# Two decode layers on one core: the weights and cache in 76 loads instead of 90

## The chip, the cores and the metric

The kernel runs on one core of a Trainium2 chip. The metric is the device time of one execution in microseconds (us); before the change it is 732.17 us, the median of 3 runs (731.61 to 732.62). A matrix unit (PE, with its weight loads listed as PEld), a vector engine (DVE), a scalar engine (ACT) and the queue engine SP, which only issues loads here, each work through their own instructions in order and wait for each other on semaphores.

## What is computed

Four tokens (one for each of 4 sequences) pass an attention layer and a gated MLP, and then the same two again with the same weights and the same cache:

```
x = x + A(layernorm(x));  x = x + B(layernorm(x))      # and once more
A: q = x @ wq                      # 640 -> 32 heads of 128
   k, v = last 1024 cached rows    # 4 x 32 heads x 1024 x 128, fp32
   o = softmax(q k^T / sqrt(128)) v;   return o @ wo
B: g = x @ W_gate; g = g * (g > 0);   return (g * (x @ W_up)) @ W_down   # 640 -> 1728 -> 640
```

Everything is fp32. Each layer needs all 32 heads' keys and values (each head's 4096 columns of 128 rows of either), the projections and the MLP's 25,920 columns; only what fits on chip is kept from the first layer to the second.

## The kernel before

The host lays the data out as three arrays of 128 rows. `heads` holds, in the order of use, the query weights ("q"), keys ("k"), values ("v") and output weights ("o") of heads 0 to 26; `kept` holds those of heads 27 to 31, as 3,200 columns of "o", 3,200 of "q" (the kept W_q) and 40,960 of keys and values; `mlp` holds the MLP's weights: 1,920 columns for the last piece of gate and up weights, three blocks of 5,120 for the rest, and then the down weights. A column is 512 bytes over the 128 rows.

On chip there is one buffer `store` of 50,624 columns and a small `first_q` for the first 4,288 columns of `heads`. A list `plan` is written out by hand in `decode_kernel`: every entry says which layer it is for, from which array, which columns, and where in `store` they go. `load()` takes the next entry as soon as the kernel's text has passed the last use of the columns that it overwrites, and issues one load on SP's queue (L221). On the chip, that load waits until the last instruction that uses any of its target columns is done. So a load of two pieces in one waits for the later of their two release times, and who uses it waits until all of it has landed.

The order of the work: layer 1 goes through the common heads in groups of four (last, a group of three), and then through the kept heads (27 to 31). The kept keys and values stay in `store`, where layer 2 starts with them, so that while the first MLP and the start of layer 2 run, only a narrow part of `store` is free: 3,264 columns behind the kept ones (from `FRONT`), and three small stretches (`AHEAD`, `AWAY`, `BACK`), whose kept contents are moved aside to PSUM and small tiles for that time. The first MLP's loads go round these places, layer 2's first loads also; as layer 2 works off the kept heads, the places behind them come free, and the loads grow ("first stretch", L182 to L199). Then come loads of about 15,872 columns round `store` (`stretch`), the last heads, and the second MLP, cut in `cuts` (L204).

In an MLP (`forward`), `gate(3)` multiplies with the 1,920 columns, `gate(0)` to `gate(2)` with a block of 5,120 each, and `gated(j)` makes one block's hidden values on ACT and DVE, for which the next block's matmuls wait. `down(3)`, `down(0)`, `down(1)`, `down(2)` follow; each multiplies one hidden block with 640 columns at a time. All matmuls with loaded data are issued by `product` (L252). `normalized` makes the layer norm and the turned input xT, with a few idle matmuls (`busy`, `fill`) beside it; in the second layer's MLP, there are none after `gate(3)`.

Of the kernel before, what the change touches and what calls it, by code (L numbers as in the profile page):

```python
# [13 lines left out]
B, D, H, DH, W, F = 4, 640, 32, 128, 1024, 1728  # L14
# [12 lines left out]
KV = 4096  # L27
# [4 lines left out]
KEPT = len(HEADS[K0]) + len(HEADS[K1])  # L32
# [19 lines left out]
GU0, GU = KC * 3 * P, KC * 4 * 256  # L52
WD0 = GU0 + 3 * GU
TAIL, WD1, WD = WD0 + D, WD0 + D + 2 * QUARTER, 4 * D
MLP = WD1 + 3 * WD
# [6 lines left out]
STORE = 50624  # L62
FRONT = KEPT * 2 * (D + KV)


AHEAD = KEPT * D, KEPT * D + 768
BACK = FRONT - 2 * KV - 1728, FRONT - 2 * KV
AWAY = BACK[0] - 1280, BACK[0]
HOME = 12864
FIRST, MOST = 32640, 16320  # L70
# [7 lines left out]
def fewest(lo, end, n):  # L78

    if n == 1:  # L80
        return (0, [end]) if end - lo <= MOST else (n + len(CUTS), [])
    most = min(lo + MOST, end)
    ends = [(most, most not in CUTS)] + [(x, False) for x in CUTS if most - 512 < x < most]
    return min((fewest(hi, end, n - 1)[0] + cut, [hi, *fewest(hi, end, n - 1)[1]]) for hi, cut in ends)


def spread(parts):


    at, places, cuts = 0, {}, [0]  # L90
    for what, i in parts:
        places[what, i] = at
        size = size_of(what, i)
        step = {"q": size // KC, "k": 512, "v": 512, "o": D}[what]
        cuts += range(at + step, at + size + 1, step)
        at += size
    return places, at, cuts


ROWS = {row: spread(parts) for row, parts in PARTS.items()}  # L100

CUTS = frozenset(ROWS["heads"][2])
fewest = cache(fewest)
WHERE = {part: (row, at) for row, (places, _, _) in ROWS.items() for part, at in places.items()}

# [2 lines left out]
def decode_kernel(ctx: ExitStack, tc: tile.TileContext, x, source, sel, out):  # L108
    nc = tc.nc
# [10 lines left out]
    store = big.tile([P, STORE], F32, name="store")  # L120
# [9 lines left out]
    def put(layer, row, to, *cuts):  # L130

        for lo, hi in zip(cuts, cuts[1:]):
            assert 0 < hi - lo <= MOST and to % 64 == lo % 64 == hi % 64 == 0 and to + hi - lo <= STORE, (row, lo, hi, to)
            plan.append((layer, row, lo, hi, to))
            to += hi - lo
        return to

    def stretch(layer, lo, end, to):

        for hi in fewest(lo, end, -(-(end - lo) // MOST))[1]:  # L140
            if to + hi - lo > LAP:
                to = 0
            to = put(layer, "heads", to, lo, hi)
            lo = hi
        return to

    def at_part(what, i):
        return WHERE[what, i][1]

    def near(c, row="heads"):  # L150

        return max(x for x in ROWS[row][2] if x <= c)

    heads_end = ROWS["heads"][1]
    k0, v0 = at_part("k", HEADS[K0][0]), at_part("v", HEADS[K0][0])
    k1, v1 = at_part("k", HEADS[K1][0]), at_part("v", HEADS[K1][0])


    q_end = 2 * KEPT * D
    turn = min(c for c in ROWS["heads"][2] if c >= heads_end - (STORE - q_end))  # L160
    mid = [near(turn + (heads_end - turn) * i // 3) for i in (1, 2)]
    to = stretch(0, HELD, turn, FIRST)
    assert to <= KEPT * D or to > 2 * MOST, to
    put(0, "kept", KEPT * D, KEPT * D, q_end)
    put(0, "heads", q_end, turn, *mid, heads_end)
    put(0, "kept", k0, k0, k1, v0, v0 + 6656, v1, v1 + KV, v1 + 7168, FRONT)
    put(0, "kept", 0, 0, len(HEADS[K0]) * D, KEPT * D)


    f, z, a, q, k = FRONT, STORE - D, AHEAD[0], AWAY[0], BACK[0]  # L170
    assert STORE - FRONT == 2 * 1280 + 64 + D
    gu = [(z, D), (f, 1280), (f + 1280, 1344), (a, 768), (k, 960), (k + 960, 768), (q, 1280)]
    gu_end = [(f, 1280), (f + 1280, 1280), (f + 2560, D)]
    wd = [(a, D), (k, 960), (k + 960, D), (q, 1280), *gu_end, (a, D), (k, D), (k + D, D)]
    lo = 0
    for to, n in gu + gu + gu_end + wd:
        put(0, "mlp", to, lo, lo + n)
# [2 lines left out]


    lo = HELD  # L182
    for to, n in (f, 1280), (f + 1280, 1280), (f + 2560, D + 64), (a, 768), (k, 1728):
        put(1, "heads", to, lo, lo + n)
        lo += n
    to = AHEAD[1]
    for n in 1152, 1280, 1024, 2048, 3392:
        to = put(1, "heads", to, lo, lo + n)
        lo += n
    assert to == HOME  # L190
    to = HOME + BACK[1] - BACK[0]
    for n in 4096, 6144, 9728:
        hi = near(lo + n)
        to = put(1, "heads", to, lo, hi)
        lo = hi
    hi = near(lo + 4608)
    to = put(1, "heads", to, lo, hi)
    lo, hi = hi, near(hi + STORE - to)
    put(1, "heads", to, lo, hi)  # L199
    last = near(heads_end - 25216)  # L200
    to = stretch(1, hi, last, 0)
    for lo, hi in (last, near(last + 12800)), (near(last + 12800), heads_end):
        to = put(1, "heads", to if to + hi - lo <= STORE else 0, lo, hi)
    cuts = [0, 7040, 12160, GU0 + 3 * GU, WD1 + WD, MLP - 4 * D, MLP - 2 * D, MLP - D, MLP]  # L204
    for lo, hi in zip(cuts, cuts[1:]):
        to = put(1, "mlp", to if to + hi - lo <= STORE else 0, lo, hi)

# [2 lines left out]
    live = [False] * STORE  # L210
    held = {}

    def load():

        if not held:
            nc.sync.dma_start(out=first_q, in_=source["heads"][:, :HELD])
        while plan and not any(live[plan[-1][4]:plan[-1][4] + plan[-1][3] - plan[-1][2]]):
            layer, row, lo, hi, to = plan.pop()
            live[to:to + hi - lo] = [True] * (hi - lo)
            held.setdefault((layer, row), []).append((lo, hi - lo, to))  # L220
            nc.sync.dma_start(out=store[:, to:to + hi - lo], in_=source[row][:, lo:hi])  # L221

    def free(a, b):
        live[a:b] = [False] * (b - a)
        load()
# [29 lines left out]
    def done(layer, row, lo, n):  # L255

        if row == "kept" and layer == 0:
            return
        if row == "kept":
            for p in range(lo, lo + n):  # L260
                if BACK[0] <= p < BACK[1]:
                    live[HOME + p - BACK[0]] = False
                elif not (AHEAD[0] <= p < AHEAD[1] or HOME <= p < HOME + BACK[1] - BACK[0]):
                    live[p] = False
        else:
            for first, m, p in held[key(layer, row)]:
                a, b = max(lo, first) - first, min(lo + n, first + m) - first
                if a < b:
                    live[p + a:p + b] = [False] * (b - a)
        load()  # L270
# [8 lines left out]

    probs = work.tile([P, W], F32, name="probs")  # L280
    load()
    gates = work.tile([P, 512], F32, name="gates")
    sel_sb = const.tile([P, P + 32], F32, name="sel_sb")
# [390 lines left out]
```

## Time and profile before

| | |
|---|---|
| median of 3 runs | 732.17 us (731.61 to 732.62) |
| profiled execution, first to last instruction (its span) | 729.8 us |
| bytes read | 310.57 MB |
| loads on SP's queue | 90, and one store |
| PE busy, share of the span | 60% |
| mean granted PE clock | 0.822 |

The profile gives no other time of the profiled execution than its span, 729.8 us; the median of the timed runs lies 2.3 us above it, for what the span does not hold. The tables of the profile give busy times by engine, the chain of waits that ended last, and, for chosen stretches of time, the busy time of each engine, the granted PE clock and the rate of the loads.

### The profile page before, as it was taken

The page shows a single profiled execution, that of the slowest core. Times are in us where ns is not written, and L with a number is a line of the kernel's source. Part 1 is how long each engine was busy: PE and PEld are TensorE (multiplying, and loading weights), DVE is VectorE, ACT ScalarE, POOL GpSimd, SP SyncE. Part 2 cuts the span into 40 slices and gives each one's busy share as a digit, 9 for nine tenths or more (in the row PEclk, how much of TensorE's full clock was granted, in tenths as well). Part 3 has the DMA queues.
Part 4 walks back from the last instruction along what each step waited for, and adds up shares of the span by engine and source line. Part 5 has one row for each costly group of instructions (what it writes and reads, how often), then busy time and mean ns, then how long its engine had stood idle before and what let it go on. Part 6 is the DMA issues. An engine that isn't in the chain of part 4 may idle for free.

```text
span 729.8 us, 8270 instructions
## 1 busy us (share of the span) xinstructions
PE 437.2 (60%) x3764; PEld 143.9 (20%) x3764; DVE 76.7 (11%) x277; ACT 54.2 (7%) x101; POOL 0.3 (0%) x5
## 2 busy tenths in 40 slices
PE   0745565555646664619868896365656556555575
PEld 0211111111111111103333241021111112111132
DVE  1111001010010101001111211001010010101011
ACT  0200000000000000000412210000000000000100
POOL 0000000000000000000000000000000000000000
PEclk9888888876777777759999999677777777878899
DMA  9999999999999999999999999999999999999996
GB/s 409 442 398 443 442 443 416 438 440 439 418 439 432 411 460 421 447 416 426 419 407 401 434 429 449 445 425 435 425 435 443 429 434 427 441 433 430 421 425 289
DMA packets 13290, 311.17 MB, mean 426 GB/s; under 512 B 1476, under 2 KB 1732, under 8 KB 6984
## 3 DMA queue, kind: packets, MB, share of 16 engines
q1 hardware_dynamic: 13104, 310.56, 99.0%
q8 instruction: 29, 0.48, 0.2%
q10 hardware_dynamic: 152, 0.09, 0.1%
q14 instruction: 5, 0.04, 0.0%
HBM read 310.57 MB, written 0.08 MB: 426 GB/s over the span
## 4 chain that ended last, share of the span: by engine, by line
DMA 76%; PE 21%; another core or an unknown queue 1%; DVE 1%; issue 1%; SPq 0%; ACT 0%; DVEq 0%; ACTq 0%
DMA store<-in_heads 60%; PE ps L252 9%; DMA store<-in_kept 8%; DMA store<-in_mlp 7%; PE po L252 5%; PE m L252 2%; PE y L252 1%; PE pp L252 1%; PE pp L432 1%; PE m L403 1%; PE m L472 0%; PE m L463 0%; PE m L345 0%; PE y L375 0%
## 5 line engine op out<-in xcount | busy, mean ns | idle before, releaser
L252 PE MATMUL po<-store,pT 128*16 128x512 f32 (+1 forms) x1026 | 155.3, 709 | 123.6 <-DMA store<-in_heads 118.2
L252 PE MATMUL ps<-store,qT 128*4 128x512 f32 (+4 forms) x996 | 150.4, 684 | 109.8 <-DMA store<-in_heads 89.2
L252 PEld LDWEIGHTS po<-store,pT 128*16 128x16 f32 x1026 | 34.2, 109 | 230.3 <-issue 109.2
L252 PEld LDWEIGHTS ps<-store,qT 128*4 128x4 f32 x996 | 29.9, 93 | 213.4 <-DMA store<-in_heads 100.3
L424 DVE TENSOR_REDUCE nm<-ps 128x1 f32<-128x1024 f32 x17 | 20.8, 1225 | 240.7 <-PE ps L252 240.7
L428 ACT ACTIVATE probs<-ps,nm 128x1024 f32<-128x1024 f32 x17 | 18.9, 1114 | 327.0 <-DVE nm L424 327.0
L252 PE MATMUL m<-store,xT 128*32 128x512 f32 (+4 forms) x150 | 28.4, 570 | 11.0 <-DMA store<-in_heads 11.0
L442 DVE COPY pT<-pp 128x16 f32<-128x16 f32 x128 | 17.1, 169 | 137.8 <-PE po L252 137.8
L252 PE MATMUL y<-store,oT 128*4 128x160 f32 x514 | 22.6, 307 | 9.9 <-DMA store<-in_heads 8.7
L459 ACT COPY gates<-po 128x512 f32<-128x512 f32 x16 | 9.4, 587 | 252.4 <-PE po L252 252.4
L252 PE MATMUL pp<-store,xT 128*32 128x256 f32 (+3 forms) x322 | 20.1, 350 | 8.7 <-DMA store<-in_mlp 4.3
L432 PE MATMUL pp<-sel_sb,probs 128*128 128x128 f32 x144 | 20.7, 291 | 0.0
L465 DVE RECIPROCAL r<-m 128x16 f32<-128x16 f32 x18 | 4.6, 258 | 132.9 <-PE m L463 132.9
L432 PEld LDWEIGHTS pp<-sel_sb,probs 128*128 128x128 f32 x144 | 18.3, 153 | 0.0
L252 PEld LDWEIGHTS y<-store,oT 128*4 128x4 f32 x514 | 12.7, 88 | 17.5 <-DMA store<-in_heads 9.1
L396 DVE TENSOR_SCALAR gates<-m,rstd 128x512 f32<-128x512 f32 (+2 forms) x18 | 12.4, 690 | 24.9 <-PE m L252 24.9
L252 PEld LDWEIGHTS pp<-store,xT 128*32 128x32 f32 x322 | 10.3, 109 | 17.0 <-DMA store<-in_mlp 7.7
L472 PE MATMUL m<-sel_sb,gates 128*128 128x128 f32 x72 | 11.9, 287 | 0.8 <-DVE gates L452 0.8
L403 PE MATMUL m<-sel_sb,gates 128*128 128x128 f32 x64 | 12.3, 315 | 0.0
L322 PE MATMUL y<-probs,sel_sb 4*4 4x160 f32 x8 | 0.7, 444 | 18.2 <-DMA sel_sb<-in_sel 18.2
L403 PEld LDWEIGHTS m<-sel_sb,gates 128*128 128x128 f32 x64 | 7.6, 155 | 18.3 <-issue 17.9
L252 PE MATMUL y<-store,gates 128*4 128x160 f32 x192 | 9.6, 299 | 2.5 <-DMA store<-in_mlp 2.3
(74 smaller groups left out, 126.1 us busy)
## 6 DMA issues: line engine op xcount, KB each, us to landing
store<-in_heads SPq DMA_DIRECT2D x17, 7936.0 KB, 46.1
store<-in_heads SPq DMA_DIRECT2D x2, 8160.0 KB, 44.7
store<-in_heads SPq DMA_DIRECT2D x2, 8128.0 KB, 36.1
store<-in_heads SPq DMA_DIRECT2D x2, 7968.0 KB, 36.1
store<-in_heads SPq DMA_DIRECT2D x1, 8096.0 KB, 26.4
store<-in_heads SPq DMA_DIRECT2D x1, 7424.0 KB, 44.9
store<-in_heads SPq DMA_DIRECT2D x1, 7360.0 KB, 35.8
store<-in_heads SPq DMA_DIRECT2D x1, 7168.0 KB, 34.0
```

The lines of the kernel that those rows point to most:

```text
L252: nc.tensor.matmul(out[:, a:z], by, t[rows, p:p + z - a], start=start and not a, stop=stop and z == n, **how)
L322: nc.tensor.matmul(y[32 * g:32 * g + B], ident[:B, :B], probs[:B, g * QUARTER:(g + 1) * QUARTER], start=True, stop=True, tile_position=(0, ...
L396: nc.vector.tensor_scalar(gates[:, :len(HEADS[g]) * P], qp.pop(g), rstd, SCALE, op0=ALU.mult, op1=ALU.mult)
L403: nc.tensor.transpose(qt[:, i], gates[:, i * P:(i + 1) * P], ident)
L424: nc.vector.tensor_reduce(nm[g], to.rearrange("p j n -> p (j n)"), axis=AX.X, op=ALU.max, negate=True)
L428: nc.scalar.activation(probs, sc.pop(g).rearrange("p j n -> p (j n)"), AF.Exp, bias=nm.pop(g), accum_out=sums[g])
L432: nc.tensor.transpose(pp[:, c // 4, c % 4 * P:c % 4 * P + P], probs[:, c * P:(c + 1) * P], ident)
L442: nc.vector.tensor_copy(to[:, 4 * j:4 * j + 4], pp[:, j].rearrange("p (c x) -> p c x", c=4)[:, :, i:P:32])
L459: nc.scalar.copy(gates, po)
L465: nc.vector.reciprocal(r[g], so.rearrange("p (b i) -> p i b", b=B)[:, :SIDE])
L472: nc.tensor.transpose(ot[:, 127 * b:127 * b + P], gates[:, b * P:(b + 1) * P], ident)
```

## The change

Three groups of loads are put together; no byte more or less is read, and no arithmetic changes.

1. The kept W_q (3,200 columns) were a load of their own in layer 1. Now the host also writes them into the array `heads`, in front of the load of the last common heads at `turn`, and that load brings both. The three loads there become nearly equal.
2. The first MLP is loaded in 19 pieces instead of 27 (640 + 1,280 columns become 1,920, 960 + 768 become 1,728, and so on), and layer 2's first stretch in 11 instead of 15.
3. The second MLP's first cut falls away: the 1,920 columns and the first two blocks of 5,120 come in one load of 12,160 columns, instead of 7,040 and 5,120. The last heads' loads of layer 2 are cut at other columns, four as before.

```
+QUERIES = min(c for c in CUTS if c >= ROWS["heads"][1] - (STORE - 2 * KEPT * D)), KEPT * D
...
-    put(0, "kept", KEPT * D, KEPT * D, q_end)
     put(0, "heads", q_end, turn, *mid, heads_end)
-    put(0, "kept", k0, k0, k1, v0, v0 + 6656, v1, v1 + KV, v1 + 7168, FRONT)
+    put(0, "kept", k0, k0, k1, v0, v0 + 6656, v1, v1 + 5120, v1 + 7168, FRONT)
...
-    gu = [(z, D), (f, 1280), (f + 1280, 1344), (a, 768), (k, 960), (k + 960, 768), (q, 1280)]
-    gu_end = [(f, 1280), (f + 1280, 1280), (f + 2560, D)]
-    wd = [(a, D), (k, 960), (k + 960, D), (q, 1280), *gu_end, (a, D), (k, D), (k + D, D)]
+    gu = [(f, 1920), (f + 1920, 1344), (a, 768), (k, 1728), (q, 1280)]
+    gu_end = [(f, 1920), (f + 1920, 1280)]
+    wd = [(a, D), (k, 1600), (q, 1280), *gu_end, (a, D), (k, 1280)]
...
-    for n in 1152, 1280, 1024, 2048, 3392:
+    for n in 2432, 3072, 3392:
...
-    for n in 4096, 6144, 9728:
+    for n in 4096, 8192:
...
-    hi = near(lo + 4608)
+    hi = near(lo + 12288)
...
-    last = near(heads_end - 25216)
-    to = stretch(1, hi, last, 0)
-    for lo, hi in (last, near(last + 12800)), (near(last + 12800), heads_end):
+    to = stretch(1, hi, turn, 0)
+    last, end = near(turn + MOST), near(heads_end - 12608)
+    for lo, hi in (turn, last), (last, end), (end, heads_end):
...
-    cuts = [0, 7040, 12160, GU0 + 3 * GU, WD1 + WD, MLP - 4 * D, MLP - 2 * D, MLP - D, MLP]
+    cuts = [0, GU0 + 2 * GU, GU0 + 3 * GU, WD1 + WD, MLP - 4 * D, MLP - 2 * D, MLP - D, MLP]
...
-            nc.sync.dma_start(out=store[:, to:to + hi - lo], in_=source[row][:, lo:hi])
+            at, n = lo, hi - lo
+            if row == "heads" and lo >= QUERIES[0]:
+                at += QUERIES[1]
+            if (layer, row, lo) == (0, "heads", QUERIES[0]):
+                at, n, to = at - QUERIES[1], n + QUERIES[1], to - QUERIES[1]
+                assert to == KEPT * D and n <= MOST and not any(live[to:to + QUERIES[1]])
+                live[to:to + QUERIES[1]] = [True] * QUERIES[1]
+                held.setdefault((layer, "kept"), []).append((to, QUERIES[1], to))
+            nc.sync.dma_start(out=store[:, to:to + n], in_=source[row][:, at:at + n])
```

SP's queue in layer 2's first stretch, before (line, operation, target and source, rows x columns):

```order
L221 DMA store<-in_heads 128x1728
L221 DMA store<-in_heads 128x1152
L221 DMA store<-in_heads 128x1280
L221 DMA store<-in_heads 128x1024
L221 DMA store<-in_heads 128x2048
L221 DMA store<-in_heads 128x3392
L221 DMA store<-in_heads 128x4096
L221 DMA store<-in_heads 128x6144
L221 DMA store<-in_heads 128x9728
L221 DMA store<-in_heads 128x4608
L221 DMA store<-in_heads 128x11264
```

The same place with the change:

```order
L230 DMA store<-in_heads 128x1728
L230 DMA store<-in_heads 128x2432
L230 DMA store<-in_heads 128x3072
L230 DMA store<-in_heads 128x3392
L230 DMA store<-in_heads 128x4096
L230 DMA store<-in_heads 128x8192
L230 DMA store<-in_heads 128x12288
L230 DMA store<-in_heads 128x11264
```

Two pairs are now one load each, and three loads (6,144, 9,728 and 4,608 columns) have become two; the load of 12,288 columns ends where that of 4,608 ended, in the array and in `store`, and so waits for the same last use.

SP's queue at the end of layer 2, before, from the second last pair of large loads on:

```order
L221 DMA store<-in_heads 128x16320
L221 DMA store<-in_heads 128x15936
L221 DMA store<-in_heads 128x12800
L221 DMA store<-in_heads 128x12672
L221 DMA store<-in_mlp 128x7040
L221 DMA store<-in_mlp 128x5120 x2
L221 DMA store<-in_mlp 128x3520
L221 DMA store<-in_mlp 128x2560
L221 DMA store<-in_mlp 128x1280
L221 DMA store<-in_mlp 128x640 x2
```

With the change:

```order
L230 DMA store<-in_heads 128x13824
L230 DMA store<-in_heads 128x15872
L230 DMA store<-in_heads 128x15360
L230 DMA store<-in_heads 128x12672
L230 DMA store<-in_mlp 128x12160
L230 DMA store<-in_mlp 128x5120
L230 DMA store<-in_mlp 128x3520
L230 DMA store<-in_mlp 128x2560
L230 DMA store<-in_mlp 128x1280
L230 DMA store<-in_mlp 128x640 x2
```

The last load of heads is the same 12,672 columns, the one ahead of it reaches back further, and the MLP's first two loads are one.

PE in the second layer's MLP, before, with the semaphores that each row waits for: DMAHW and a number is the landing of a load, DVE and Activation are steps of those engines. Rows of 32x128 are `gate(3)`, rows of 32x256 `gate(0)`, `gate(1)` and `gate(2)`:

```order
L252 MATMUL pp<-store,xT 32x128 [waits DMAHW4_49,DVE_49]
L252 MATMUL pp<-store,xT 32x128 x14
L345 MATMUL m_109<-ones,sel_sb 32x1 [waits Activation_49]
L345 MATMUL m_109<-ones,sel_sb 32x1 x3
L375 MATMUL y<-probs,sel_sb 128x160
L252 MATMUL pp<-store,xT 32x256 [waits DVE_49]
L252 MATMUL pp<-store,xT 32x256 x19
L566 MATMUL m_108<-sel_sb,gates 64x4 x4
L252 MATMUL pp<-store,xT 32x256 [waits DMAHW5_49,DVE_49]
L252 MATMUL pp<-store,xT 32x256 x19
L252 MATMUL pp<-store,xT 32x256 [waits DMAHW6_49,DVE_49]
L252 MATMUL pp<-store,xT 32x256 x19
```

With the change:

```order
L261 MATMUL pp<-store,xT 32x128 [waits DMAHW7_49,DVE_49]
L261 MATMUL pp<-store,xT 32x128 x14
L354 MATMUL m_109<-ones,sel_sb 32x1 [waits Activation_49]
L354 MATMUL m_109<-ones,sel_sb 32x1 x3
L384 MATMUL y<-probs,sel_sb 128x160
L261 MATMUL pp<-store,xT 32x256 [waits DVE_49]
L261 MATMUL pp<-store,xT 32x256 x19
L575 MATMUL m_108<-sel_sb,gates 64x4 x4
L261 MATMUL pp<-store,xT 32x256 [waits DVE_49]
L261 MATMUL pp<-store,xT 32x256 x19
L261 MATMUL pp<-store,xT 32x256 [waits DMAHW0_49,DVE_49]
L261 MATMUL pp<-store,xT 32x256 x19
```

The order of the matmuls is the same; `gate(1)` has lost its own wait for a load, and the wait in front of `gate(3)` is now for the load that also brings the blocks of `gate(0)` and `gate(1)`.

More of the change, by code (lines that the diff above doesn't have):

```diff
@@ L160, in decode_kernel @@
     turn = min(c for c in ROWS["heads"][2] if c >= heads_end - (STORE - q_end))
-    mid = [near(turn + (heads_end - turn) * i // 3) for i in (1, 2)]
+    mid = [near(turn + (heads_end - turn + QUERIES[1]) * i // 3 - QUERIES[1]) for i in (1, 2)]
+    assert (turn, q_end - KEPT * D) == QUERIES
     to = stretch(0, HELD, turn, FIRST)
     assert to <= KEPT * D or to > 2 * MOST, to
-    put(0, "kept", KEPT * D, KEPT * D, q_end)
     put(0, "heads", q_end, turn, *mid, heads_end)
-    put(0, "kept", k0, k0, k1, v0, v0 + 6656, v1, v1 + KV, v1 + 7168, FRONT)
+    put(0, "kept", k0, k0, k1, v0, v0 + 6656, v1, v1 + 5120, v1 + 7168, FRONT)
     put(0, "kept", 0, 0, len(HEADS[K0]) * D, KEPT * D)
-    f, z, a, q, k = FRONT, STORE - D, AHEAD[0], AWAY[0], BACK[0]
+    f, a, q, k = FRONT, AHEAD[0], AWAY[0], BACK[0]
     assert STORE - FRONT == 2 * 1280 + 64 + D
-    gu = [(z, D), (f, 1280), (f + 1280, 1344), (a, 768), (k, 960), (k + 960, 768), (q, 1280)]
-    gu_end = [(f, 1280), (f + 1280, 1280), (f + 2560, D)]
-    wd = [(a, D), (k, 960), (k + 960, D), (q, 1280), *gu_end, (a, D), (k, D), (k + D, D)]
+    gu = [(f, 1920), (f + 1920, 1344), (a, 768), (k, 1728), (q, 1280)]
+    gu_end = [(f, 1920), (f + 1920, 1280)]
+    wd = [(a, D), (k, 1600), (q, 1280), *gu_end, (a, D), (k, 1280)]
     lo = 0
@@ L182, in decode_kernel @@
     lo = HELD
-    for to, n in (f, 1280), (f + 1280, 1280), (f + 2560, D + 64), (a, 768), (k, 1728):
+    for to, n in (f, 1920), (f + 1920, 1344), (a, 768), (k, 1728):
         put(1, "heads", to, lo, lo + n)
@@ L637 @@
     laid = {row: np.concatenate([parts[what][i] for what, i in row_of], axis=1) for row, row_of in PARTS.items()}
+    at, size = QUERIES
+    queries = laid["kept"][:, KEPT * D:KEPT * D + size]
+    laid["heads"] = np.concatenate([laid["heads"][:, :at], queries, laid["heads"][:, at:]], axis=1)
     n = 3 * 512
```

## The prediction

> **What bounds the kernel now.** I read the page first: queues, bytes, and the chain that ended last.
>
> ```profile
> q1 hardware_dynamic: 13104, 310.56, 99.0%
> HBM read 310.57 MB, written 0.08 MB: 426 GB/s over the span
> DMA 76%; PE 21%; another core or an unknown queue 1%; DVE 1%; issue 1%; SPq 0%; ACT 0%; DVEq 0%; ACTq 0%
> ```
>
> The loads' packets fill 99.0% of the 16 DMA engines' time. So the span is the bytes over their rate, plus what is lost where the rate is below its best, plus what follows the last load. The bytes don't change. Next I asked for stretches: the first MLP with the first issues of layer 2 (366 to 396 us), the rest of the narrow part of `store` (396 to 450), and the large loads (450 to 660). The columns are the stretch, its length, busy time of PE, PEld, DVE, ACT and POOL, the granted PE clock, the DMA share, and GB/s.
>
> ```profile
> 366.00:396.00 30.00, 23.16 (x327) 11.41 (x326) 2.90 (x11) 3.55 (x10) 0.00 (x0) 1.00 1.02 406
> 396.00:450.00 54.00, 50.71 (x496) 18.89 (x492) 13.09 (x40) 10.19 (x19) 0.00 (x0) 1.00 1.02 429
> 450.00:660.00 210.00, 115.01 (x838) 33.36 (x838) 16.18 (x62) 7.75 (x13) 0.00 (x0) 0.76 1.00 434
> ```
>
> Large loads run at 434 GB/s. The stretch of small ones reaches 406, though its engines count as fully busy (1.02): what is lost there goes into the loads themselves, not into an empty queue. The loss is 30 x (1 - 406/434) = 1.94 us, and in the 54 us after it 54 x (1 - 429/434) = 0.62 us. Their sum, 2.56 us, is the most that these two stretches have to give. Last I read the chain's end.
>
> ```profile
> 656.85 38.68 DMA store<-in_heads
> ...
> 695.60 30.68 DMA store<-in_mlp
> ...
> 726.32 0.50 PE y L252 x8
> ...
> 726.85 0.33 DVE probs L615
> ```
>
> The last heads land at 656.85 + 38.68 = 695.53, the last weights at 726.28; then PE needs 0.50 us for the last 640 columns. The end is the queue's end, as long as PE has everything else done by then.
>
> **The change part by part.** *Fourteen loads fewer* (one for the kept W_q, 8 in the first MLP, 4 in the first stretch, one in the second MLP). What one costs can be read from small loads that land one after another:
>
> ```profile
> 371.15 7.42 DMA store<-in_mlp
> ...
> 388.52 7.08 DMA store<-in_mlp
> ...
> 395.65 0.50 PE y L252 x8
> ```
>
> The first row is the load that ends at column 12,032 of `mlp`, landing at 378.57; the second is the last, column 25,920, landing at 395.60. Between them lie 13,888 columns of 512 bytes, 7.11 MB, in 17.03 us and 15 loads. At 434 GB/s they take 16.38 us; the rest is 0.65 us, or 43 ns a load. The other bound is the whole 1.94 us of the stretch over its 26 loads, 75 ns; below, I see no reason why fewer loads should cost queue time by themselves, so 0. I take 43, from landings rather than from a stretch cut through loads: 14 x 0.043 = **0.60 us gained** (0 to 1.05). In the Trainium skill, "DMA: Bandwidth & Descriptors" (Anatomy of one DMA) fits about 2.0 us of fixed cost to each DMA; by that the sum would be 28 us. The rows above disagree, as here the fixed part passes behind the loads ahead of it.
>
> *Later issue.* A merged load waits for the later of two releases, and an empty queue would cost more than the 43 ns. The rows: SP's issues, landings by size, and the smallest transfer of all.
>
> ```profile
> 392.18 1.77 SPq L221 DMA_DIRECT2D store<-in_heads  x2
> 412.91 0.33 SPq L221 DMA_DIRECT2D store<-in_heads  x1
> store<-in_heads SPq DMA_DIRECT2D x1, 3072.0 KB, 14.2
> 426.76 0.33 SPq L221 DMA_DIRECT2D store<-in_heads  x1
> out_x<-probs SPq DMA_DIRECT2D x1, 80.0 KB, 1.6
> store<-in_heads SPq DMA_DIRECT2D x1, 7360.0 KB, 35.8
> ```
>
> A transfer lands 1.6 us after its issue with nothing ahead of it, so a load that is issued with 1.6 us or more still queued leaves no gap. Tightest are two places. The first load of layer 2 went out at 392.18; with 640 columns more to wait for (0.50 us of matmuls as above, some 0.7 with the idle ones between) it goes at 392.9 to 393.2, when the queue ends at 395.60 - 0.5 = 395.1: 1.9 us. The load of 12,288 columns waits for what the one of 4,608 waited for, 426.76. Ahead of it is the load of 8,192, which ends 2,048 columns (2.42 us) behind the one of 6,144 that landed at 412.91 + 14.2 = 427.1, less the 0.55 saved: 429.0, so 2.2 us. Both hold, narrowly: 0. Without that cover, up to 1.6 us each. The PE rows for the last 640 columns also double, as they now come as 1,280: 0.5 us later after the landing, which comes 0.5 earlier; so layer 2 starts when it did. The kept W_q: the large loads there land 35.8 us after issue, of which 17 are their own; waiting some us more for room costs nothing, and PE uses the queries one group later.
>
> *The second MLP's first load.* Here PE waits anew. Its rows in the profiled order:
>
> ```profile
> 706.15 0.49 PE L336 MATMUL po<-sel_sb 128*128 128x128 f32 x2
> 707.11 1.18 PE L252 MATMUL pp<-store,xT 128*32 128x128 f32 x27 [0.47 <-DVE xT L359]
> 709.72 2.37 PE L252 MATMUL pp<-store,xT 128*32 128x256 f32 x40 [0.81 <-DVE gates L555]
> 712.96 2.37 PE L252 MATMUL pp<-store,xT 128*32 128x256 f32 x40 [0.54 <-DVE probs L555]
> 716.20 2.37 PE L252 MATMUL pp<-store,xT 128*32 128x256 f32 x40 [0.88 <-DVE probs L555]
> 720.15 0.84 PE L252 MATMUL y<-store,probs 128*4 128x160 f32 x16 [1.58 <-DMA store<-in_mlp]
> 720.91 1.27 PE L252 MATMUL y<-store,gates 128*4 128x160 f32 x32
> 723.35 1.27 PE L252 MATMUL y<-store,gates 128*4 128x160 f32 x32 [1.16 <-DMA store<-in_mlp]
> 724.89 1.11 PE L252 MATMUL y<-store,gates 128*4 128x160 f32 x24 [0.28 <-DMA store<-in_mlp]
> ```
>
> `gate(3)` starts at 707.11, waiting for xT, not for a load. With the change it waits for 12,160 columns, 6.23 MB, 14.35 us behind the last heads: 709.88, so it starts 2.8 us later, at 709.92. Its followers wait for DVE steps of the block before and shift along: blocks at 712.5, 715.8 and 719.0, the last ending at 721.4 instead of 718.57. Behind them stand the waits for loads: 1.58 us before 720.15, 1.16 before 723.35, 0.28 before 724.89. They add up to 3.0, against 2.8. So at an unchanged clock PE is just in time, with **0.2 us** to spare.
>
> The clock is what is not unchanged. Between 706.64 and 709.92 PE has nothing to do, 3.3 us, which it never had there before. Stretches of 3.41 us, the grid in which this trace's clock changes:
>
> ```profile
> 190.40:193.81 3.41, 1.38 (x4) 0.11 (x2) 0.00 (x0) 0.00 (x0) 0.00 (x0) 1.00 1.19 507
> 193.81:197.22 3.41, 0.00 (x0) 0.00 (x0) 0.00 (x0) 0.00 (x0) 0.00 (x0) 0.50 0.83 358
> 282.56:285.97 3.41, 1.73 (x14) 0.22 (x6) 0.19 (x2) 0.88 (x2) 0.00 (x0) 1.00 0.98 419
> 285.97:289.38 3.41, 0.00 (x0) 0.00 (x0) 0.00 (x0) 0.00 (x0) 0.00 (x0) 1.00 0.96 414
> 606.82:610.24 3.42, 2.57 (x16) 0.51 (x17) 0.00 (x0) 0.00 (x0) 0.00 (x0) 0.50 1.07 464
> 610.24:613.65 3.41, 3.41 (x14) 1.01 (x7) 0.24 (x1) 0.58 (x1) 0.00 (x0) 0.50 0.82 354
> 613.65:617.06 3.41, 3.41 (x36) 1.82 (x38) 1.04 (x4) 0.00 (x0) 0.00 (x0) 1.00 1.16 503
> 702.40:705.81 3.41, 2.29 (x31) 1.14 (x30) 1.04 (x4) 0.37 (x1) 0.00 (x0) 1.00 0.99 425
> 709.22:712.64 3.42, 2.70 (x48) 1.51 (x48) 0.45 (x3) 0.50 (x2) 0.00 (x0) 1.00 1.01 436
> ```
>
> A stretch with PE busy 1.38 of 3.41 us is followed by half clock, one with 1.73 is not; at half clock, 2.57 was not enough to come back, 3.41 was. Wherever the grid falls, the gap leaves one stretch near or below 1.38: if it lies whole in one, 0.1; if split in the middle, 1.8 us of work at the shares of 702.40 (0.67) and 709.22 (0.79), 1.2 and 1.4. So I expect half clock behind the gap. Blocks of 2.37 then take 4.74 and the 0.87 between them stays, so a stretch at half clock is 84% busy, 2.9 us, and does 1.44 us worth of work: it loses 1.44, less the 0.2 to spare: **1.24 us lost**. Bounds: 0, if the clock stays, and 2.7 us, if a second stretch stays at half.
>
> *Sum.* Against the profiled span: 729.8 - 0.60 + 0 + 1.24 = 730.5. The median of the runs lies 2.3 us above that span, and I carry that over: 732.17 + 0.64 = **732.8 us**.
>
> **The rivals.** *The clock stays.* Then the end is the queue's end, 0.60 us earlier: 731.6. For it: 3.3 us is a bare stretch of the grid. Against it: the row of 190.40. In the Trainium skill, "TensorE: Matmul & The Clock Gate" (HAM oscillation) warns of idle gaps over about 3.4 us only, and by that this rival would be the outcome; the trace lowered the clock behind a stretch that was not idle throughout. 17%.
>
> *Two stretches at half clock* (the other side, slower). If the low stretch begins inside the gap, it isn't busy enough to end it, as at 606.82, and the next stays at half too: 2 x 1.44 - 0.2 = 2.7 lost, 732.17 - 0.60 + 2.7 = 734.3. It decides from where the grid's edge falls more than some 0.8 us ahead of 709.92 (2.57 of 3.41 busy is too little). The same page (What's actually happening) says that the grid runs free of the kernel's start; by that the two cases would alternate between executions. 27%.
>
> *The narrow queue runs dry.* If layer 2's loads are released 1 us later than I reckon, or the queue is 1 us shorter, one of the two tight places costs its share of 1.6 us, with the clock's loss on top: about 733.6. For it: covers of 1.9 and 2.2 us over 1.6. Against: none of the 15 loads there left a hole worth more than the 0.62 us of 396 to 450. 8%.
>
> *The stretches give all.* If what the two stretches lose is loads that wait for one straggling engine, and larger loads cure it, 2.56 us are gained; with the clock staying, 729.6. For it: 406 against 434 is more than 43 ns a load explains (26 x 0.043 = 1.1 of 1.94). Against: most of those loads stay. 13%.
>
> **How the numbers follow.** One stretch at half clock, my forecast, has 35%: 732.8. A measurement of this kernel can tell about 0.2%, or 1.46 us: 730.7 to 733.6 counts as no change. That holds the forecast, the staying clock and a quarter of the dry queue's 8%: 35 + 17 + 2 = 54%, and 2% of the stretches' 13% where they give less: 56%. Faster keeps 11%; slower has 27 + 6 = 33%. The range leaves out most of the stretches' gain and the case of two half-clock stretches with a dry queue: 731.0 to 734.8.
>
> **What would show it.** Right: loads of layer 2 leave no stretch under 400 GB/s between 392 and 432; `gate(3)` waits about 2.8 us for `store<-in_mlp`, a window near 709 to 716 is granted 0.50, and the matmuls 128x256 there take twice their time. The last landing lies about 31 us behind the last heads' in both; if it comes 0.6 us sooner in absolute time and PE ends late, the sum is right. Wrong: a clock of 1.00 throughout the second MLP, or a last landing that moved by more than 1.1 us either way.

## The result and the profile after

The kernel with the change takes 735.65 us, the median of 6 runs (733.27 to 737.67), against 732.04 us for the one before, also 6 runs (731.61 to 732.62). The ratio is 1.0049 (95% interval 1.0039 to 1.0059): slower by 3.6 us. The profiled execution of the changed kernel took 734.99 us with a span of 733.1, which is 3.3 more than the span before. Single runs take 1.8 to 1.9 us longer than their spans, so the profiled execution before is the run of 731.61 us, the fastest of its six; part of the 2.3 us between its span and the median is the spread of the runs.

The page of the changed kernel gives the same bytes in fewer packets, at a lower mean rate.

```profile
q1 hardware_dynamic: 11088, 310.56, 98.7%
HBM read 310.57 MB, written 0.08 MB: 424 GB/s over the span
```

Its end, from the chain of waits:

```profile
673.99 38.41 DMA store<-in_mlp
712.40 0.14 issue
712.54 1.94 PE pp L261 x25
...
726.11 4.07 PE y L261 x112
730.21 0.33 DVE probs L624
```

The load of 12,160 columns lands at 673.99 + 38.41 = 712.40. Before, the same last column landed at 709.90, so the queue is 2.5 us behind here (landings without a row are those of the trace's DMA records). The last weights land at 728.87, 2.6 us later than before (726.28). And PE isn't through 0.5 us after that landing, as it was: DVE takes over at 730.21 instead of 726.85, 3.36 us later. So **2.6 us are lost in the queue of loads and 0.8 us at its end, on PE.**

For the queue, the three stretches that were shown of before, now with the change:

```profile
366.00:396.00 30.00, 22.05 (x312) 11.22 (x315) 3.16 (x11) 3.55 (x10) 0.00 (x0) 1.00 0.99 394
396.00:450.00 54.00, 47.98 (x466) 17.69 (x460) 11.23 (x33) 8.98 (x17) 0.00 (x0) 1.00 1.01 416
450.00:660.00 210.00, 118.67 (x868) 33.82 (x862) 18.06 (x69) 8.97 (x15) 0.00 (x0) 0.78 1.00 435
```

The large loads run as before (435 GB/s), and the narrow part of `store` is slower: 394 for 406 and 416 for 429. That is 30 x 12/434 + 54 x 13/434 = 2.4 us, nearly all of the queue's loss. Two short stretches hold most of it: first before, then with the change.

```profile
392.00:400.00 8.00, 7.03 (x106) 3.19 (x103) 1.77 (x5) 2.46 (x6) 0.00 (x0) 1.00 1.01 386
425.00:432.00 7.00, 7.00 (x90) 3.25 (x86) 0.93 (x1) 0.00 (x0) 0.00 (x0) 1.00 0.97 417
```

```profile
392.00:400.00 8.00, 7.27 (x116) 3.30 (x115) 1.72 (x5) 2.04 (x5) 0.00 (x0) 1.00 0.91 317
425.00:432.00 7.00, 7.00 (x75) 2.95 (x77) 0.90 (x2) 0.00 (x0) 0.00 (x0) 1.00 1.01 393
```

These are the two places that the prediction had called the tightest. A window of 7 us holds only some 80 packets, so its rate is coarse. Counted instead by the bytes that have moved, in the trace's DMA records, the changed kernel is 0.1 us behind the one before at 392 us, 1.6 at 400, 1.5 at 420 and 2.7 at 440: about 1.5 us are lost at the first place and 1.2 at the second. The busy share of the 16 DMA engines in 40 slices of 385 to 400 us (0.375 us each), before and then with the change, shows the hole itself:

```profile
DMA  9999999999999999999999999998999999999999
```

```profile
DMA  9999999989999999999999963895979999957779
```

From 393.6 us on the engines run empty: the tenths fall to 6 and 3, and again to 5 some 4 us later. SP's issues of the changed kernel around it, and at the second place:

```profile
393.74 3.18 SPq L230 DMA_DIRECT2D store<-in_heads  x4
...
427.19 0.33 SPq L230 DMA_DIRECT2D store<-in_heads  x1
```

The first load of layer 2 went out at 393.74, 1.6 us later than before (392.18), and 1.78 us before the last load ahead of it had landed (395.52). Its first packet starts at 394.70, 1.0 us after the issue, and its packets take up to 1.39 us where most take 0.29. At the second place the issue, at 427.19, lies 3.7 us before the landing of the load ahead of it (430.91).

For PE, the stretches of 3.41 us around the gap, cut where the clock changes in this trace, at 711.57 and 718.39 (PE, PEld, DVE, ACT, POOL, clock, DMA share, GB/s), and PE's rows:

```profile
708.16:711.57 3.41, 0.84 (x12) 0.46 (x10) 0.87 (x3) 0.72 (x3) 0.00 (x0) 1.00 0.89 385
711.57:714.98 3.41, 2.44 (x39) 2.46 (x39) 0.00 (x0) 0.00 (x0) 0.00 (x0) 0.50 0.95 407
714.98:718.39 3.41, 2.99 (x26) 1.44 (x30) 0.44 (x2) 0.57 (x2) 0.00 (x0) 0.50 0.98 419
718.39:721.81 3.42, 2.87 (x56) 1.58 (x52) 0.76 (x3) 0.37 (x1) 0.00 (x0) 1.00 1.01 425
```

```profile
712.54 2.14 PE L261 MATMUL pp<-store,xT 128*32 128x128 f32 x27 [3.46 <-DMA store<-in_mlp]
...
716.20 3.42 PE L261 MATMUL pp<-store,xT 128*32 128x256 f32 x40 [0.42 <-DVE gates L564]
...
720.50 2.37 PE L261 MATMUL pp<-store,xT 128*32 128x256 f32 x40 [0.55 <-DVE probs L564]
723.75 2.37 PE L261 MATMUL pp<-store,xT 128*32 128x256 f32 x40 [0.87 <-DVE probs L564]
725.93 0.84 PE L261 MATMUL y<-store,probs 128*4 128x160 f32 x16
726.70 3.44 PE L261 MATMUL y<-store,gates 128*4 128x160 f32 x96
```

`gate(3)` now waits 3.46 us, and for `store<-in_mlp` as forecast. A stretch with PE busy 0.84 of 3.41 us is followed by two at half clock: `gate(3)` takes 2.14 us instead of 1.18, `gate(0)` 3.42 instead of 2.37. The last 112 matmuls run without a wait for any load, so at the end PE is the late one.

### The profile page after: what moved, and what is told of

Its sections match the earlier page's. It is cut to its first block, busy times and chain, and to the rows that moved or that the text cites. A ratio compares the mean times of both kernels' runs of the same rounds, so it can differ in the third digit from the quotient of the medians.

```text
span 733.1 us, 8211 instructions
## 1 busy us (share of the span) xinstructions
PE 442.5 (60%) x3748; PEld 144.6 (20%) x3748; DVE 76.7 (10%) x277; ACT 54.2 (7%) x101; POOL 0.3 (0%) x5
## 4 chain that ended last, share of the span: by engine, by line
DMA 76%; PE 22%; DVE 1%; issue 1%; ACT 0%; SPq 0%; DVEq 0%
DMA store<-in_heads 59%; DMA store<-in_kept 9%; PE ps L261 8%; DMA store<-in_mlp 8%; PE po L261 5%; PE pp L261 3%; PE m L261 2%; PE y L261 2%; PE pp L441 1%; PE m L412 0%; DVE nm L433 0%; PE m L481 0%; PE m L472 0%; PE po L338 0%; PE m L354 0%
## 5 line engine op out<-in xcount | busy, mean ns | idle before, releaser
L261 PE MATMUL po<-store,pT 128*16 128x512 f32 (+1 forms) x1026 | 159.3, 721 | 118.2 <-DMA store<-in_heads 112.4
L261 PE MATMUL ps<-store,qT 128*4 128x512 f32 (+1 forms) x988 | 151.8, 689 | 103.7 <-DMA store<-in_heads 82.6
L261 PE MATMUL pp<-store,xT 128*32 128x256 f32 (+3 forms) x314 | 21.6, 384 | 12.1 <-DMA store<-in_mlp 8.7
L261 PEld LDWEIGHTS m<-store,xT 128*32 128x32 f32 x150 | 6.3, 115 | 31.7 <-issue 17.8
L481 PE MATMUL m<-sel_sb,gates 128*128 128x128 f32 x72 | 11.5, 279 | 0.8 <-DVE gates L461 0.8
```

What stands on the lines that cost most here:

```text
L261: nc.tensor.matmul(out[:, a:z], by, t[rows, p:p + z - a], start=start and not a, stop=stop and z == n, **how)
L481: nc.tensor.transpose(ot[:, 127 * b:127 * b + P], gates[:, b * P:(b + 1) * P], ident)
```

## The experiments

Every kernel was timed against the kernel before, whose median was 731.96 to 732.05 us in these series.

### Layer 2's first stretch as before, the cut as before, the clock kept up

The first theory put the queue's loss on layer 2's own larger loads and the rest on the new wait before `gate(3)`. *First stretch*: the changed kernel with layer 2's first stretch loaded in its 15 old pieces.

```diff
-    for to, n in (f, 1920), (f + 1920, 1344), (a, 768), (k, 1728):
+    for to, n in (f, 1280), (f + 1280, 1280), (f + 2560, D + 64), (a, 768), (k, 1728):
-    for n in 2432, 3072, 3392:
+    for n in 1152, 1280, 1024, 2048, 3392:
-    for n in 4096, 8192:
+    for n in 4096, 6144, 9728:
-    hi = near(lo + 12288)
+    hi = near(lo + 4608)
```

> Layer 2's first stretch is loaded in the 15 pieces of before; all else as changed (80 loads). If the holes in the queue there cost the 2.5 us by which the last heads land later (698.1 against 695.5 us in the profiles), they land at about 695.1 here, and what stays is the half clock at the end: 732.4 to 734. If the loss comes from elsewhere (engines that straggle behind instruction fetches, say), the last heads still land near 698 and the time stays near 735.6.

Measured: 734.27 us (733.76 to 735.82), ratio 1.0033 (1.0021 to 1.0045). Only 1.4 of the 3.6 us come back.

*The cut*: the changed kernel with the second MLP cut as before, so that `gate(3)` waits for 7,040 columns.

```diff
-    cuts = [0, GU0 + 2 * GU, GU0 + 3 * GU, WD1 + WD, MLP - 4 * D, MLP - 2 * D, MLP - D, MLP]
+    cuts = [0, GU0 + GU, GU0 + 2 * GU, GU0 + 3 * GU, WD1 + WD, MLP - 4 * D, MLP - 2 * D, MLP - D, MLP]
```

> The second MLP's first load is cut as before (7,040 and 5,120 columns); all else as changed (77 loads). If the gap in front of the first gate and the half clock behind it cost what the profile shows, PE is done with the last weights 0.5 us after they land again, the clock stays at 1.00 behind 700 us, and the time falls by 0.8 to 1.9 us, to 733.8 to 734.8, with less spread between runs. If the end is the queue's alone, nothing changes: 735.6. The last heads land near 698 in both.

Measured: 735.33 us (733.92 to 736.51), ratio 1.0043 (1.0031 to 1.0055). In its profile `gate(3)` waits for xT again and PE ends 0.5 us behind the last landing, but the median falls by only 0.3 us, less than the two intervals can tell apart.

*The clock kept up*: the changed kernel with idle matmuls before `gate(3)` in layer 2.

```diff
+        if layer:
+            fill(12)
```

> As changed, but with 12 idle matmuls of 128 columns in front of the second layer's first gate, in the gap where PE waits for the load (76 loads). If the half clock is what the gap costs, the windows from 709 us on are granted 1.00, the gates' matmuls take their usual time though they start as late as in the changed kernel, and the time falls by 0.8 to 1.9 us to 733.8 to 734.8. If it is the late start itself, nothing is gained: 735.6.

Measured: 735.58 us (734.65 to 737.89), ratio 1.0050 (1.0038 to 1.0062). Two stretches of the time in which the changed kernel stood at 0.50, and the first two blocks:

```profile
711.82:715.24 3.42, 2.21 (x20) 2.02 (x19) 0.00 (x0) 0.04 (x1) 0.00 (x0) 1.00 0.98 421
715.24:718.65 3.41, 2.33 (x52) 1.93 (x56) 0.44 (x2) 0.57 (x2) 0.00 (x0) 1.00 0.93 398
```

```profile
710.86 3.17 PE L345 MATMUL po<-sel_sb 128*128 128x128 f32 x26
715.52 1.18 PE L261 MATMUL pp<-store,xT 128*32 128x128 f32 x27 [1.49 <-DMA store<-in_mlp]
...
718.12 2.37 PE L261 MATMUL pp<-store,xT 128*32 128x256 f32 x40 [0.81 <-DVE gates L564]
```

With idle matmuls in the gap the clock stays at 1.00 and the blocks take 1.18 and 2.37 us again. So the gap is what lowered the clock. But the median does not move. The clock's cost is real in the profile and small beside what the queue loses: runs of one kernel that lie 3.2 us (here) and 4.4 us apart (the changed kernel) don't show 0.8 us.

*Both undone*: first stretch and cut as before; the kept W_q, the first MLP in 19 loads and the new cuts of the last heads' loads remain.

> Both undone: what stays of the change is the kept W_q with the common heads and the first MLP in 19 loads (81 loads). If the two causes are all that made it slower, this is faster than before by 9 x 0.043 = 0.4 us: 731.6. If larger loads in the first MLP cost something too, 732.5 or more.

Measured: 734.0 us (732.85 to 736.68, 11 runs), ratio 1.0027 (1.0018 to 1.0035). The first theory falls: 2 us are still lost with both of its causes gone. The profile says where:

```profile
393.25 6.65 SPq L230 DMA_DIRECT2D store<-in_heads  x6
```

```profile
392.00:400.00 8.00, 7.18 (x116) 3.39 (x116) 1.57 (x5) 1.90 (x5) 0.00 (x0) 1.00 0.92 322
```

The hole is still there (322 GB/s) with layer 2's loads in their old pieces. What is left is that the first of them goes out at 393.25. So the cause is to be looked for ahead of it, in what releases its place.

### What releases layer 2's first load

That load's place (`FRONT`) still holds down weights of the first MLP. PE's rows on them, before and then with the change (8 matmuls are 640 columns):

```profile
391.02 0.46 PE L252 MATMUL y<-store,gates 128*4 128x160 f32 x8 [0.34 <-DMA store<-in_mlp]
...
391.66 0.45 PE L252 MATMUL y<-store,gates 128*4 128x160 f32 x8
```

```profile
391.94 0.46 PE L261 MATMUL y<-store,gates 128*4 128x160 f32 x8 [0.74 <-DMA store<-in_mlp]
...
392.58 0.46 PE L261 MATMUL y<-store,gates 128*4 128x160 f32 x8
...
393.23 0.46 PE L261 MATMUL y<-store,gates 128*4 128x160 f32 x8
```

The piece of 1,920 columns lands 0.92 us after the one of 1,280 did, because all of it has to land, and then takes 0.65 us more to work off. Together 1.57 us, and the issue moved by 1.56. The second theory is therefore: the merged *down weights* cause the loss, and a late issue costs time because a load takes longer to start than the queue ahead of it lasts. Its rival: the size of layer 2's own loads.

*Queries and gates alone*: kept W_q, new cut of the last common heads and merged gate and up pieces as in the changed kernel; down weights, first stretch and cut as before (85 loads).

```diff
-    gu_end = [(f, 1920), (f + 1920, 1280)]
-    wd = [(a, D), (k, 1600), (q, 1280), *gu_end, (a, D), (k, 1280)]
+    gu_end = [(f, 1280), (f + 1280, 1280), (f + 2560, D)]
+    wd = [(a, D), (k, 960), (k + 960, D), (q, 1280), *gu_end, (a, D), (k, D), (k + D, D)]
```

> Of the change there stay the kept W_q, the new cuts of the last heads and the merged gate and up pieces of the first MLP; the down weights' pieces, layer 2's first stretch and the last MLP are cut as before (85 loads). If the merged down weights delay layer 2's first load until the queue in front of it is shorter than the time that a load takes to start, that delay is gone: the first load goes out near 392.2 us again, no hole between 394 and 400 us, and 5 loads fewer give 731.6 to 732.2. If the loss sits in the other merges or in stragglers, it stays near 734.

Measured: 732.23 us (731.46 to 733.71, 11 runs), ratio 1.0004 (0.9995 to 1.0013): nothing lost. It differs from the kernel above with both undone in these two lines only, and they are worth 1.7 us (each kernel against the one before in its own series).

```profile
392.53 7.10 SPq L230 DMA_DIRECT2D store<-in_heads  x6
```

```profile
392.00:400.00 8.00, 7.08 (x108) 3.01 (x107) 1.77 (x5) 2.17 (x5) 0.00 (x0) 1.00 1.00 379
```

*Down weights alone*: the kernel before with these two lines as in the changed one, and nothing else.

> The kernel before with the merged down weights of the first MLP alone (gu_end and wd, 86 loads). If they are the cause of the hole, layer 2's first load goes out about 1 us later than before, near 393.2 us, the loads from 394 to 400 us lose 1.3 us or more on the mean of the engines, and the time is 733.2 to 734. If not: 731.9.

Measured: 734.32 us (734.18 to 736.08), ratio 1.0035 (1.0023 to 1.0048): 2.4 us slower.

```profile
395.61 4.51 SPq L221 DMA_DIRECT2D store<-in_heads  x5
```

```profile
392.00:400.00 8.00, 7.83 (x114) 3.64 (x113) 0.36 (x2) 1.74 (x4) 0.00 (x0) 0.99 0.80 264
```

Layer 2's first load, with its old 1,280 columns, goes out at 395.61, and the rate falls to 264. Here some of the MLP's own last loads are late too: the last one lands at 397.44. This profiled execution is the slowest of the five (736.08 us; the others took 734.18 to 734.80), and its clock stands at half from 385.38 to 392.20 us, which slows PE's work on the down weights besides. So the 2.4 us rest on the median, and the rows of this kernel show the late issue larger than it is in its other runs.

*Larger first loads alone*: the kernel before with the first three loads of layer 2 in two.

```diff
-    for to, n in (f, 1280), (f + 1280, 1280), (f + 2560, D + 64), (a, 768), (k, 1728):
+    for to, n in (f, 1920), (f + 1920, 1344), (a, 768), (k, 1728):
```

> The kernel before with layer 2's first three loads made two (1,920 and 1,344 columns, 89 loads) and nothing else. Released 0.7 us later than before with 2.7 us of queue in front of it instead of 3.4. If a load takes 1.6 us to start, as the store at the end does, nothing is lost: 732.0. If it takes 2.3 to 2.6 us, as the first load of the program does, and more on the engines that are ahead, 0.5 to 1 us is lost: 732.5 to 733.

Measured: 732.65 us (732.31 to 733.18, 11 runs), ratio 1.0008 (0.9999 to 1.0017).

```profile
393.04 7.16 SPq L221 DMA_DIRECT2D store<-in_heads  x6
```

```profile
392.00:400.00 8.00, 7.03 (x109) 3.13 (x102) 1.77 (x5) 2.41 (x6) 0.00 (x0) 1.00 0.94 351
```

The load of 1,920 waits for 640 columns more and goes out 0.86 us later, as the prediction had reckoned; even that, with 2.63 us to the landing ahead of it, lowers the rate to 351. These are the very sizes of the changed kernel, and they lose 0.7 us, with an interval from -0.1 to 1.2. As the whole cause the rival is too small.

*First piece small again*: the kernel with both undone, but `FRONT`'s first pieces 1,280 and then one large one, in the down weights and in layer 2.

```diff
-    gu_end = [(f, 1920), (f + 1920, 1280)]
+    gu_end = [(f, 1280), (f + 1280, 1920)]
-    for to, n in (f, 1280), (f + 1280, 1280), (f + 2560, D + 64), (a, 768), (k, 1728):
+    for to, n in (f, 1280), (f + 1280, 1984), (a, 768), (k, 1728):
```

> The merged first MLP with layer 2's first stretch and the last MLP as before, but in the down weights behind FRONT the small piece first (1,280 then 1,920 columns instead of 1,920 then 1,280), and layer 2's first loads cut alike (1,280 then 1,984): 80 loads, one fewer than the version with both undone (734.0). If the release time of layer 2's first load is what counts, and not the number or size of loads, it goes out near 392.2 us again and most of the 2 us comes back: 731.8 to 732.6. If merging as such costs, it stays near 734.

Measured: 733.78 us (732.47 to 735.23, 11 runs), ratio 1.0027 (1.0018 to 1.0036). The gain that I expected did not come. SP's first issue, its second, and the stretch:

```profile
392.27 7.88 SPq L230 DMA_DIRECT2D store<-in_heads  x5
```

```profile
395.43 0.33 SPq L230 DMA_DIRECT2D store<-in_heads  x1
```

```profile
392.00:400.00 8.00, 6.12 (x105) 2.90 (x98) 1.32 (x5) 1.65 (x5) 0.00 (x0) 1.00 0.93 342
```

The first load is as early as before, but the one behind it waits for the large piece until 395.43, so the hole has moved one load on. A queue needs its lead at every load, not at the first.

*Finer*: queries and gates alone, with layer 2's first three loads in five of 640 to 704 columns (87 loads).

```diff
-    for to, n in (f, 1280), (f + 1280, 1280), (f + 2560, D + 64), (a, 768), (k, 1728):
+    for to, n in (f, D), (f + D, D), (f + 1280, D), (f + 1920, D), (f + 2560, D + 64), (a, 768), (k, 1728):
```

> The version that came back to the time before (kept W_q and merged gate and up pieces), with layer 2's first loads cut finer: 640 columns each instead of 1,280, 1,280 and 704 (87 loads). If earlier release is what the queue lacks there, the 0.5 us or more that are lost at that place even before come back, less 0.1 us for the two loads: 731.5 to 731.9. If a piece costs more than it gives: 732.3 or more.

Measured: 731.86 us (731.65 to 732.90, 11 runs), ratio 0.9996 (0.9987 to 1.0005). The rate from 392 to 400 is 385 GB/s. The time lies in the range that was expected, but the interval includes no change against before, so a gain from smaller steps is not shown.

Together, one execution each, with the loss in those 8 us against 434 GB/s, 8 x (1 - rate/434); the landing is that of the first MLP's last load on the last of the 16 DMA engines. *The cut alone* and *large end* come further down; the first has the program of before up to this place, the second that of the changed kernel:

| kernel | first issue of layer 2 | landing ahead | between | GB/s, 392 to 400 | lost, us |
|---|---|---|---|---|---|
| before | 392.18 | 395.61 | 3.43 | 386 | 0.9 |
| the cut alone | 392.46 | 395.89 | 3.43 | 365 | 1.3 |
| queries and gates alone | 392.53 | 395.92 | 3.39 | 379 | 1.0 |
| finer | 392.64 | 396.69 | 4.05 | 385 | 0.9 |
| larger first loads alone | 393.04 | 395.67 | 2.63 | 351 | 1.5 |
| first stretch | 393.23 | 395.75 | 2.52 | 315 | 2.2 |
| both undone | 393.25 | 395.78 | 2.53 | 322 | 2.1 |
| large end | 393.63 | 395.42 | 1.79 | 329 | 1.9 |
| changed | 393.74 | 395.52 | 1.78 | 317 | 2.2 |
| down weights alone | 395.61 | 397.44 | 1.83 | 264 | 3.1 |

The loss goes with the time between issue and landing and not with the size of the loads: with 2.5 us, 1,280 columns lose 2.1 and 2.2, and with 2.6 us 1,920 lose 1.5. With 3.4 us or more it is 0.9 to 1.3, of which 0.4 is the difference between two executions of the same program; with 2.5 us and less it is about 2, and no larger for 1.8 than for 2.5. (The last kernel loses in the MLP's own loads as well, within the same 8 us.) All kernels with 2.5 us or less have the merged down weights, so that these cost time through the late issue is argued from the rows; *larger first loads alone* is the one test of a late issue without them.

### The second place, the cut by itself, the price of one load

*Large end*: the changed kernel with 4,096, 6,144, 9,728 and 4,608 columns for its 4,096, 8,192 and 12,288 (77 loads).

```diff
-    for n in 4096, 8192:
+    for n in 4096, 6144, 9728:
-    hi = near(lo + 12288)
+    hi = near(lo + 4608)
```

> As changed, but with the large end of layer 2's first stretch in the pieces of before (4,096, 6,144, 9,728, 4,608, 77 loads). If the load of 12,288 columns is issued too late, the 1.3 us that are lost ahead of it come back: 734.0 to 734.6. If the queue had enough in front of it: 735.6.

Measured: 734.49 us (732.99 to 736.23), ratio 1.0034 (1.0021 to 1.0046): 1.2 us back by the medians, though the interval overlaps with that of the changed kernel (1.0039 to 1.0059). The rate at the second place is 428 GB/s instead of 393:

```profile
425.00:432.00 7.00, 7.00 (x79) 3.03 (x81) 0.90 (x2) 0.00 (x0) 0.00 (x0) 1.00 1.00 428
```

Counted by the bytes that have moved, this kernel is 1.3 us behind the one before at 420 us and still at 440, where the changed one goes from 1.5 to 2.7. The two other kernels with the load of 12,288 columns (the cut, the clock kept up) lose 1.3 and 1.0 us there, and none of those without it more than 0.1. So the second place's loss belongs to these merged loads. How the late issue costs it stays open: the engines hardly run empty (0.4 us on the mean of the 16, from 425 to 432), but the packets of the load of 12,288 columns take up to 3.44 us where most take 1.82.

*The cut alone*: the kernel before with `cuts = [0, 12160, ...]` (89 loads).

> The kernel before with the second MLP's first load of 12,160 columns and nothing else (89 loads). If the half clock behind the gap is worth what I forecast, 1.2 us with up to 2.7, then 732.8 to 734.5, and PE ends over 0.5 us behind the last landing. If it is hidden behind the last loads: 732.0.

Measured: 732.89 us (732.03 to 735.62, 11 runs), ratio 1.0017 (1.0007 to 1.0027), so 0.9 us slower (0.5 to 2.0).

```profile
708.52:711.93 3.41, 1.51 (x40) 1.52 (x40) 0.10 (x1) 0.26 (x3) 0.00 (x0) 1.00 0.94 402
711.93:715.35 3.42, 2.76 (x26) 1.21 (x29) 0.44 (x2) 0.49 (x2) 0.00 (x0) 0.50 0.98 420
715.35:718.76 3.41, 2.86 (x60) 1.53 (x53) 0.76 (x3) 0.37 (x1) 0.00 (x0) 1.00 0.99 415
```

One stretch at half clock, just what was forecast; but in this execution PE caught up and ended 0.5 us behind the last landing. So the profile shows the clock fall and not its cost, and where the 0.9 us of the median arise stays open. Counted by bytes, the queue of this execution falls 0.6 us behind that of the kernel before between 392 and 405 us, where both programs are the same: single executions differ by that much without any change.

*One load more*: the kernel before with every load of heads over 12,000 columns issued as two halves, 29 loads more.

```diff
+            cut = near(lo + (hi - lo) // 2) if row == "heads" and hi - lo > 12000 else hi
-            nc.sync.dma_start(out=store[:, to:to + hi - lo], in_=source[row][:, lo:hi])
+            nc.sync.dma_start(out=store[:, to:to + cut - lo], in_=source[row][:, lo:cut])
+            if cut < hi:
+                nc.sync.dma_start(out=store[:, to + cut - lo:to + hi - lo], in_=source[row][:, cut:hi])
```

> The kernel before with every load of heads over 12,000 columns issued as two halves, 29 loads more (119), all in places where the queue has 16 MB or more in front. It measures what a load costs by itself: at 43 ns 1.25 us more, 733.2; at the upper bound of 75 ns 734.1; at nothing 732.0.

Measured: 733.37 us (732.98 to 733.72, 11 runs), ratio 1.0018 (1.0009 to 1.0027): 1.34 us for 29 loads, 46 ns each (23 to 68 by the interval).

## Why the prediction was wrong, step by step

**The step that failed is "Later issue", put at 0.** It said that a load issued with 1.6 us or more still queued leaves no gap, and took both tight places for safe; they cost 1.5 and 1.2 us. That 1.6 was the row of the small store, which moves 80 KB out of the chip. A row nearer to these loads stood in the DMA view of before, the load that starts the kernel in an empty queue:

```profile
first_q<-in_heads SPq DMA_DIRECT2D x1, 2144.0 KB, 7.7
```

4,288 columns are 2.195 MB, 5.06 us at 434 GB/s; the load lost the other 2.6 us. In the DMA records 1.0 us of them pass from its issue (0.73) to its first packet (1.74), 1.2 us over its packets, of which early ones take up to 1.50 us where most take 0.64, and 0.4 us from the end of the last packet to the landing. With 2.6 for 1.6 both covers that the prediction reckoned, 1.9 and 2.2 us, would have been short. At the first place the table bears that out: 3.4 us ahead of the slowest DMA engine were enough and 2.5 were not. At the second place it is not the whole answer. The cover there was 3.7 us in the trace and not 2.2, and 1.2 us were lost all the same. In the Trainium skill, "DMA: Bandwidth & Descriptors" (Anatomy of one DMA) gives each DMA about 2.0 us of fixed cost, measured on another way of issuing (by GpSimd, where these loads are issued by SP). As a price per load it does not hold here (46 ns); the 2.6 us that the first load lost are of its order.

**The releases were half counted.** For layer 2's first load the prediction took only the longer matmul work of 640 columns. Down weights in larger pieces also land later, by 0.92 us. So the load came at 393.74, not 392.9 to 393.2, and the queue ahead of it ended at 395.52 instead of 395.1. Larger first loads alone, where only the reckoned part holds, went out at 393.04, in the forecast's bounds, and cost 0.7 us. For the load of 12,288 columns the issue was nearly right (427.19 for 426.76); the queue ahead of it ended later than reckoned (430.91 for 429.0), the load lost 1.2 us even so, and undoing the merge gives them back.

**"The narrow queue runs dry"** was the rival that came true, with 8% and 733.6. It was tied to a release 1 us later than reckoned; the releases were 0.5 to 0.8 us late at the first place and 0.4 at the second. It also counted one place and not both.

**The sum** in the profiled executions: the last weights should have landed 0.60 us earlier and landed 2.6 later, 3.2 us of error; PE should have cost 1.24 and cost 0.8, 0.4 the other way. Forecast plus these, 0.6 + 3.2 - 0.4 = 3.4, is the measured 3.3 within rounding. By its own sign, a last landing that moved by more than 1.1 us, the prediction was wrong. Its other sign, no stretch under 400 GB/s between 392 and 432, could not decide: the kernel before has 386 from 392 to 400.

**Fourteen loads at 43 ns** was about the right price: 46 ns measured (23 to 68), on the halves of large loads. What it bought can't be seen beside the holes. At the end of the first MLP, with 8 loads fewer behind it, the last landing is 0.1 us earlier and not 0.5, in one execution each.

**The clock** fell for the reason given, and was mis-sized. The wait was forecast as 2.8 us later than before, and `gate(3)` came at 712.54, which is 2.6 us behind the forecast 709.92 because the whole queue was. Two stretches stayed low, not one, the rival's way: 2.44 of 3.41 us busy was not enough to come back. From 712.54 the forecast's 11.5 us to the end of `gate(2)` would give 724.0; it ended at 726.1, so 2.1 us were lost for 1.44. But PE had more to spare than 0.2. The sum of the waits left out the last one, and when none of them occurs, the last 112 matmuls follow each other in 4.2 us (725.93 to 730.14), where before they took 4.9 without their waits (720.15 to 726.78, less 1.16, 0.28 and 0.33). So PE had about 0.2 + 0.3 + 0.7 = 1.2 us to spare, and 0.8 to 0.9 of the 2.1 stayed. The Trainium skill, "TensorE: Matmul & The Clock Gate" (HAM oscillation), warns of gaps over about 3.4 us; the gap here, 3.46, agrees, but in the cut alone PE idled for 2.22 us, with 1.51 of 3.41 busy, and the clock fell too.

**What stays open.** The parts do not add up: down weights 2.4, larger first loads 0.7, large end 1.2 and the cut alone 0.9 make 5.2 of 3.6 us. They share the same stretch of the queue, and a hole that one makes may cover another's. Why a late issue costs 1.2 us at the second place, with 3.7 us still ahead of it, is not shown. Why the changed kernel's runs lie 4.4 us apart, those of before 1.0, was not tried. The profiles hold a candidate: in the cut, the clock kept up and the down weights alone, each profiled in a run slower than its median, the clock stands at half for 6.8 us in the first MLP (from 380.86, 376.79 and 385.38 us); before and in the profiled run of the changed kernel it does not.

## What to carry to other kernels

Merging loads on a queue that is never empty saves tens of nanoseconds each, while every merged load is released later and lands later; ask for each what is queued ahead of it at its new issue, and compare that with the start of a like load into an empty queue, not with the smallest transfer of the page. Follow the release back one step further: whoever frees the place may itself be waiting for a merged load. Where a queue runs with little lead, cut the loads by when their places come free, not by their number.

## What the runs showed of the hardware

A load from memory into an empty queue lost 2.6 us against 434 GB/s, and its first packet started 1.0 us after its issue; one more load in a full queue cost 46 ns, and an 80 KB store landed 1.6 us after its issue. The 16 DMA engines do not end a load together: for the last load of the first MLP before, the first of them ended 2.2 us ahead of the last. Behind a hole the packets of a load were slower (up to 1.39 us where most took 0.29), so that in the changed kernel a DMA share of 0.91 stands beside 317 of 434 GB/s. After stretches with PE busy 0.84 (changed kernel) and 1.51 of 3.41 us (the cut alone) the clock halved; at half clock 2.44 busy did not bring it back, 2.76 in another kernel and 2.99 did. These shares alone are no rule: in the changed kernel's trace a stretch with 1.51 busy, from 441.92 us, kept the full clock.
